# Value matmuls ahead of the output product's piece in steps 10 and 11

## The chip, the cores and the metric

The kernel runs on one core of one Trainium2 chip. The metric is the device time of one execution, in microseconds (us); lower is better. All matmuls take bf16 operands and accumulate in fp32 in PSUM; inputs and output are fp32.

## The reference

Two stages follow each other. The first is an attention between a sequence `x` (8 batches, 8 heads, 512 tokens, 64 wide) and 32 state vectors of each batch and head, in both directions. The second is a gated feed-forward layer on the 4352 rows that come out (8 batches of 512 + 32 rows, 512 wide, hidden width 1536):

```
scores  = x @ state^T / 8            a  = softmax over the 32 states
xread   = a @ state                  (512 rows a batch)
scores2 = state @ x^T / 8            a2 = softmax over the 512 tokens
sread   = a2 @ x                     (32 rows a batch)
rows    = concat(xread, sread) with the heads side by side: 4352 x 512
out     = (sigmoid(rows @ w_gate) * (rows @ w_val)) @ w_out
```

## The kernel before

The program order of each engine is written out by hand. Work is done batch by batch; `step(b, f)` is one of twelve steps of batch `b`, for `b` = 3 to 8, where `b` = 8 stands for the 256 state rows of all batches. Step `f` makes columns `128 f` to `128 f + 127` of the hidden layer:

- Gate and value matmuls (`gv_half`, L360; L363 in batch 8). `xread` is never formed. The product of the states with both weights, `SW`, is made for each batch ahead of time (`sw_six`: state matmuls, L290 and L297; copied out by `sw_cp`, L334), and a step multiplies it by the transposed attention weights `aT`: two matmuls of 512 columns for the gate half (here called G), two for the value half (V).
- `gv_th` (ScalarE, L369) takes the tanh of half the gate; `gv_glu` (VectorE, L374) makes (tanh + 1) times the value half, the glu product; the factor one half is applied at the output.
- The output product of the batch before, `o = b - 1`, is done with Winograd's form of Strassen's method: seven products of blocks instead of eight, each in two pieces a and b of six matmuls of 256 columns (`w_mm`, L437). The sums of glu blocks that it needs are made by `s_sum` (L419), on GpSimd, and one in halves on VectorE at steps 0 and 6. `w_keep` (ScalarE, L442) and `w_add` (VectorE, L445) combine the results, and `w_store` sends them out on SP's queue.
- In steps 0 and 6 TensorE also does the state matmuls for the next batch `nb`, if there is one; the attention of the next batch (`S_mm`, L152, its exponential, sums, transposes) is spread over the other steps.

The pieces that fall into each step are these, "3b4a" being piece 3b and then piece 4a:

```
order = {0: "1a", 1: "1b", 2: "2a", 3: "2b", 4: "6a", 5: "6b", 6: "5a", 7: "5b", 8: "7a7b", 9: "3a", 10: "3b4a", 11: "4b"}
```

A step's matmuls stand as G, pieces, V. In steps 0 and 6 of a batch with a next one they stand as G, V, pieces (`ahead`).

The PSUM tiles of G and V come from one pool of two buffers (`p_gv`), taken in turn, so that in a run of steps G uses one and V the other. Steps 0 and 6 take one tile of the same pool for a state product too. A gate tile is free when `gv_th` has read it, a value tile when `gv_glu` has, a state product when `sw_cp` has. The `tanh` tiles have three buffers, the glu products of a batch two.

What follows the matmuls in steps 10 and 11: `gv_glu`, then one `w_add` on VectorE and one `w_store`. In step 9 `gv_glu` is followed by a `sw_cp` on VectorE. In step 0 VectorE does `s_sum(o, 3, 0)` after `gv_glu`, and GpSimd two `s_sum` that read the glu products of the last six steps of the batch before, the eleventh among them.

Of the kernel before, what the change touches and what calls it, by code (L numbers as in the profile page):

```python
# [16 lines left out]
def kernel(  # L17
# [239 lines left out]
    def rd_mm(b, place):  # L257

        ps = place[0].tile((128, 512), FP, name="rdp", tag=place[1])
        rd = held["rd", b] = ps[:, :2 * D + 2].rearrange("p (e d) -> p e d", e=2)  # L260
        for e in range(2):
            for c in range(4):
                for j in range(4):
                    h, o, Eb = 2 * j + e, rd[j * Ns:(j + 1) * Ns, e], Ebs[b][:, c, e, j * Ns:(j + 1) * Ns]
                    if b > 2:
                        nc.tensor.matmul(o, Eb, xs[:, c, h, :D + 1], start=(c == 0), stop=(c == 3))  # L266
                    else:
                        xh = xhs[b][:, h, c] if b in xhs else xbs[b][:, c, h]
                        nc.tensor.matmul(o[:, :D], Eb, xh, start=(c == 0), stop=(c == 3))
        for e in range(2 if b < 3 else 0):  # L270
            for c in range(4):
                nc.tensor.matmul(rd[:, e, D:], Ebs[b][:, c, e], ones, start=(c == 0), stop=(c == 3))
# [60 lines left out]
    def sw_cp(b, lo, w, e, cp):  # L333
        cp(*sw_left.pop((b, lo, w, e)))  # L334
# [20 lines left out]
    def gv_half(b, f, w, place):  # L355
        n, fs = n_of(b), slice(f * 128, (f + 1) * 128)
        ps = place[0].tile((128, 512), FP, name="gvp", tag=place[1])[:, :n]
        if b < B:
            for g in range(2):
                nc.tensor.matmul(ps, SWs[b][:, g, w, fs], aTs[b][:, :, g], start=(g == 0), stop=(g == 1))  # L360
        else:
            for j in range(4):
                nc.tensor.matmul(ps, (wg, wv)[w][:, j, fs], XS[:, :, j], start=(j == 0), stop=(j == 3))  # L363
        held.setdefault(("gv", b, f), []).append(ps)

    def gv_th(b, f):

        th = held["th", b, f] = fp.tile((128, 512), FP, name="th")[:, :n_of(b)]
        nc.scalar.activation(th, held["gv", b, f][0], AF.Tanh, scale=0.5)  # L369

    def gv_glu(b, f):
        if b not in glus:
            glus[b] = fp.tile((128, NF, n_of(b)), BF, name="glu", bufs=2, padded_shape=(128, NF, 512))
        nc.vector.scalar_tensor_tensor(glus[b][:, f], held["th", b, f], 1.0, held["gv", b, f][1], ALU.add, ALU.mult)  # L374
# [53 lines left out]
    def w_mm(b, k, c):  # L428

        lhs, rhs = prod(b, k)  # L430
        key = {1: 1, 6: 1, 2: 2, 5: 5, 3: 5, 7: 7, 4: 7}[k]
        first = k == key
        if first and c == 0:
            place = OU if key in (1, 5) else SWP
            wps[key] = place[0].tile((128, 2, 256), FP, name="outp", tag=place[1])
        for i in range(NF // 2):
            nc.tensor.matmul(wps[key][:, c], lhs[:, i, c * 128:(c + 1) * 128], rhs[:, i],  # L437
                             start=(first and c == 0 and i == 0), stop=(i == NF // 2 - 1), skip_group_check=True)

    def w_keep(name, key):  # L440
        t = held["w", name] = fp.tile((128, 2, 256), FP, name=name, bufs=1)
        nc.scalar.activation(t, wps[key], AF.Copy, scale=0.5)  # L442

    def w_add(key, name, to):
        nc.vector.scalar_tensor_tensor(to, wps[key], 0.5, held["w", name], ALU.mult, ALU.add)  # L445
# [4 lines left out]
    def p_mm(k, part):  # L450
        c, lo, n = parts[part]
        lhs, rhs = prod(B - 1, k)
        if k == 7:
            wps["p", part] = p_sw.tile((128, 512), FP, name="outp", tag="swp")[:, :n]
        for i in range(NF // 2):
            nc.tensor.matmul(wps["p", part], lhs[:, i, c * 128:(c + 1) * 128], rhs[:, i, lo:lo + n],  # L456
                             start=(k == 7 and i == 0), stop=(i == NF // 2 - 1), skip_group_check=True)
# [9 lines left out]
    def w_res(b, h):  # L467
        if (b, h) not in wres:
            wres[b, h] = fp.tile((128, 2, 512), FP, name="res", bufs=3)
        return wres[b, h]  # L470
# [381 lines left out]
    def sw_six(b, v):  # L852

        if b not in SWs:
            SWs[b] = fp.tile((128, 2, 2, dff), BF, name="SW", bufs=2)
        lo = 768 * v
        for k, places in enumerate((((SWP, GV), (SWP, SWP), (OU, SWP)) if v else ((OU, GV), (SWP, AT), (SWP, SWP)))):
            pss = [p[0].tile((128, 512), FP, name="swp", tag=p[1]) for p in places]
            if k < 2:
                sw_mm(pss, b, k, lo, 512, 0)  # L860
            else:
                sw_pair(pss, b, lo + 512, 256)
            for e in range(2):
                if k < 2:
                    sw_left[b, v, k, e] = (SWs[b][:, e, k, lo:lo + 512], pss[e])
                else:
                    sw_left[b, v, k, e] = (SWs[b][:, e, :, lo + 512:lo + 768], pss[e].rearrange("p (w n) -> p w n", w=2))

    def step(b, f):

        nb, o = (b + 1 if b + 1 < B else None), b - 1
        v = f // 6
        if nb and f in (0, 6):
            if v:
                rd_mm(nb, AT)
            sw_six(nb, v)
            sw_cp(nb, v, 0, 1, act)
            sw_cp(nb, v, 2 * v, 0, act)
        ahead = nb is not None and f in (0, 6)
        gv_half(b, f, 0, GV)  # L880
        gv_th(b, f)
        if ahead:
            gv_half(b, f, 1, GV)
        todo = (order if b < B else last_order)[f]
        for k, c in zip(todo[::2], todo[1::2]):
            if b == B and k == "7":
                for part in range(3):
                    if parts[part][0] == "ab".index(c):
                        p_mm(7, part)
            else:  # L890
                w_mm(o, int(k), "ab".index(c))
        if not ahead:
            gv_half(b, f, 1, GV)
        gv_glu(b, f)

        if f == 1:
            w_keep("V1", 1)
        if f == 5:
            w_keep("U2", 1)
        if nb:  # L900
            if f in (1, 2):
                S_mm(nb, f - 1, AT)
                S_exp(nb, f - 1)
            k = {0: (1, 1), 3: (2, 0), 4: (2, 1), 6: (0, 0), 7: (1, 1), 8: (2, 1)}.get(f)
            if k:
                sw_cp(nb, v, *k, act)

        if f == 0:
            s_sum(o, 3, 0, nc.vector)
        if f == 4:  # L910
            w_add(2, "V1", w_res(o, 0)[:, :, lo_])
        if f == 6:
            s_sum(o, 3, 1, nc.vector)
        if f == 7:
            held["w", "U4"] = fp.tile((128, 2, 256), FP, name="U4", bufs=1)
            w_add(5, "U2", held["w", "U4"])
        if f == 8 and b < B:
            w_add(7, "U4", w_res(o, 1)[:, :, hi_])
        if f == 9 and b == B:
            for part in range(3):  # L920
                p_add("U4", part, 1)
        if f == 10 and b < B:
            w_add(5, "U2", w_res(o, 0)[:, :, hi_])
            w_store(o, 0, nc.sync)
        if f == 11 and b < B:
            w_add(7, "U2", w_res(o, 1)[:, :, lo_])
            w_store(o, 1, nc.sync)
        if nb:
            if f in (1, 9):
                sw_cp(nb, v, 1, 0, vec)  # L930
            if f in (2, 3):
                n_sum(nb, f - 2)
            if f == 5:
                n_mul(nb, 0, nc.vector)
                n_mul(nb, 1, nc.vector)
            if f == 6:
                rd_fin(nb)
                aT_dma(nb, 0)
                aT_dma(nb, 1)
                rd_dma(nb)  # L940

        if f == 0:
            s_sum(o, 0, 1, nc.gpsimd)
            s_sum(o, 1, 1, nc.gpsimd)
            if nb:
                cast_xs(nb, 0, 4)
                cast_xs(nb, 4, 4)
                if nb + 2 < B:
                    load_x(nb + 2, nc.sync)
        if f == 3:  # L950
            if nb:
                at_Eb(nb)
            s_sum(o, 2, 1, nc.gpsimd)
        if f == 6 and nb and nb + 1 < B:
            cast_x(nb + 1, pool, 0, 4)
            cast_x(nb + 1, pool, 4, 4)
            at_xT_dma(nb + 1)
        if f == 8 and b < B:
            for t in range(3):
                s_sum(b, t, 0, nc.gpsimd)  # L960
# [49 lines left out]
```

## Time and profile before

| | |
|---|---|
| median of 3 runs | 218.63 us (217.56 to 218.9) |
| profiled execution | 217.36 us |
| its span, first to last instruction | 215.6 us |
| granted TensorE clock | 1.000 |
| busy: TensorE / VectorE / ScalarE / GpSimd | 208.3 / 147.4 / 125.6 / 130.3 us |

The span is that of the instructions alone; the profiled execution's own time has 1.8 us around it. PE is TensorE's matmuls, PEld its weight loads, DVE is VectorE, ACT is ScalarE, POOL is GpSimd, SP the queue that issues most transfers. A row of the timeline gives the start, the duration, the engine, the line of the kernel, the operation, what it writes and reads, and how many instructions are merged into it; in brackets stands the idle time of the engine before it and what ended it. Matmuls are pipelined: a record lasts longer than the distance to the next one, so the time that a group occupies TensorE is read from one start to the next. In time, step 0 of batches 3 to 7 starts at about 77, 99, 121, 144 and 166 us of the span.

### The profile page before, as it was taken

To read this page: it belongs to the slowest core of one execution; us is meant where nothing else is said; L and a number is where in the kernel's file an instruction comes from. 1 tells how busy PE (TensorE), PEld (TensorE's weight loads), DVE (VectorE), ACT (ScalarE), POOL (GpSimd) and SP (SyncE) were. 2 spreads that over 40 slices of the span, in tenths; PEclk is the share of its full clock that TensorE was granted. 3 is DMA by queue.
4 is the path that set the end of the run, shared out by engine and by line. 5 is a ranking of instruction groups with operands and counts; after the bars stand their busy time and mean duration, and the time that the engine had idled before them with its cause. 6 is when DMAs were issued, how large, how long until landed. Compare 5 with 4: busy or idle time off the path is not lost.

```text
span 215.6 us, 5110 instructions
## 1 busy us (share of the span) xinstructions
PE 208.3 (97%) x1998; PEld 124.1 (58%) x2005; DVE 147.4 (68%) x257; ACT 125.6 (58%) x233; POOL 130.3 (60%) x131
## 2 busy tenths in 40 slices
PE   8899999999999999999999999999999999999991
PEld 2555443444454456675656565656566566788851
DVE  4987987386457559876987698778967657635411
ACT  4778876585575677745775577547763443233220
POOL 8989306269949969483959296729462909360002
PEclk9999999999999999999999999999999999999999
DMA  6999999395699253526832450236011400210053
GB/s 194 203 193 200 198 295 192 96 261 106 89 277 283 47 132 108 170 43 99 286 124 43 97 198 3 49 79 222 0 40 24 191 0 5 120 74 3 0 193 102
DMA packets 40504, 27.14 MB, mean 126 GB/s; under 512 B 23744, under 2 KB 37312, under 8 KB 40480
## 3 DMA queue, kind: packets, MB, share of 16 engines
q1 hardware_dynamic: 30080, 18.95, 31.9%
q0 software_dynamic: 10112, 7.67, 21.1%
q8 instruction: 16, 0.26, 0.5%
q10 hardware_dynamic: 288, 0.20, 0.4%
q14 instruction: 8, 0.07, 0.1%
HBM read 18.35 MB, written 8.91 MB: 126 GB/s over the span
## 4 chain that ended last, share of the span: by engine, by line
PE 91%; DVE 2%; ACT 2%; DMA 2%; issue 1%; POOL 0%; POOLq 0%; SPq 0%; DVEq 0%
PE gvp L360 25%; PE outp L437 24%; PE gvp L348 15%; PE outp L390 12%; PE gvp L363 5%; PE swp L290 3%; PE swp L297 2%; DMA xf<-in_x_dram 2%; PE Sp L152 1%; DVE glu L374 1%; PE rdp L266 1%; PE outp L456 1%; PE warm L484 1%; PE aTp L238 1%; ACT SW L334 0%
## 5 line engine op out<-in xcount | busy, mean ns | idle before, releaser
L374 DVE SCALAR_TENSOR_TENSOR glu<-th,gvp 128x512 bf16<-128x512 f32 (+1 forms) x108 | 70.5, 656 | 48.3 <-ACT th L369 18.2
L369 ACT ACTIVATE th<-gvp 128x512 f32<-128x512 f32 (+1 forms) x108 | 62.0, 576 | 57.6 <-PE gvp L360 34.2
L360 PE MATMUL gvp<-aT,SW 128*128 128x512 bf16 x240 | 64.2, 379 | 0.3
L419 POOL TENSOR_TENSOR Sm<-glu 128x768 bf16<-128x768 bf16 x24 | 39.6, 1651 | 40.3 <-DVE glu L374 27.1
L334 ACT CAST SW<-swp 128x512 bf16<-128x512 f32 x70 | 39.3, 589 | 9.2 <-PE swp L290 7.6
L348 PE MATMUL gvp<-aT,SW 128*128 128x512 bf16 x144 | 35.4, 380 | 0.1
L437 PEld LDWEIGHTS <-Sm 128*128 128x128 bf16 x276 | 27.0, 98 | 10.6
L360 PEld LDWEIGHTS <-SW 128*128 128x128 bf16 x240 | 22.5, 98 | 15.9 <-issue 3.7
L390 PE MATMUL outp<-wo,glu 128*128 128x512 bf16 x113 | 28.2, 379 | 0.4
L437 PE MATMUL outp<-tw,Sm 128*128 128x256 bf16 x204 | 27.0, 273 | 0.0
L437 PEld LDWEIGHTS <-glu 128*128 128x128 bf16 x204 | 20.0, 98 | 7.7
L348 PEld LDWEIGHTS <-SW 128*128 128x128 bf16 x144 | 13.1, 98 | 16.6 <-issue 2.1
L419 POOL TENSOR_TENSOR Sm<-Sm,glu 128x768 bf16<-128x768 bf16 x12 | 20.1, 1671 | 0.9
L437 PE MATMUL outp<-wo,glu 128*128 128x256 bf16 x144 | 19.6, 273 | 0.0
L390 PEld LDWEIGHTS <-glu 128*128 128x128 bf16 x120 | 11.4, 98 | 13.6 <-issue 0.8
L334 DVE CAST SW<-swp 128x512 bf16<-128x512 f32 x26 | 17.5, 682 | 1.7 <-PE swp L297 1.7
L121 POOL CAST xb<-xf 128x1024 bf16<-128x1024 f32 x10 | 10.6, 1088 | 10.8 <-DMA xf<-in_x_dram 9.2
L204 POOL CAST Eb<-E 128x256 bf16<-128x256 f32 x32 | 11.9, 412 | 1.9 <-ACT E L172 1.9
L363 PE MATMUL gvp<-XS,wgv 128*128 128x256 bf16 x96 | 12.6, 273 | 0.0
L419 DVE TENSOR_TENSOR Sm<-glu,Sm 128x768 bf16<-128x768 bf16 x12 | 12.4, 1032 | 0.0
L403 POOL DMA_DIRECT2D out_dram<-res x2 | 1.1, 546 | 18.4 <-ACT res L394 18.4
L255 POOL CAST xs<-xf 128x1024 bf16<-128x1024 f32 x10 | 11.4, 1170 | 0.0
(94 smaller groups left out, 219.7 us busy)
## 6 DMA issues: line engine op xcount, KB each, us to landing
out_dram<-res SPq DMA_DIRECT2D x11, 512.0 KB, 2.9
xf<-in_x_dram SPq DMA_DIRECT2D x4, 1024.0 KB, 7.3
out_dram<-res SPq DMA_DIRECT2D x9, 256.0 KB, 3.4
xf<-in_x_dram POOLq DMA_DIRECT2D x2, 1024.0 KB, 10.0
wo<-in_moe_w_out_dram POOLq DMA_DIRECT2D x3, 512.0 KB, 13.1
xf<-in_x_dram SPq DMA_DIRECT2D x4, 256.0 KB, 3.9
wgv<-in_moe_w_val_dram POOLq DMA_DIRECT2D x4, 256.0 KB, 7.2
wgv<-in_moe_w_gate_dram POOLq DMA_DIRECT2D x4, 256.0 KB, 8.3
```

Of the source, the lines that this page charges most:

```text
L121: cp(xbs[b].rearrange("p c h d -> p h c d")[:, lo:lo + n], (xhs if b in xhs else xfs)[b][:, lo:lo + n])
L204: nc.gpsimd.tensor_copy(Ebs[b][:, c], E1s[b][:, c])
L255: pool(xs.rearrange("p c h d -> p h c d")[:, lo:lo + n, :, :D], xfs[b][:, lo:lo + n])
L334: cp(*sw_left.pop((b, lo, w, e)))
L348: nc.tensor.matmul(ps, SWs[b][:, g, w, fs], aTs[b][:, :, g], start=(g == 0), stop=(g == 1))
L360: nc.tensor.matmul(ps, SWs[b][:, g, w, fs], aTs[b][:, :, g], start=(g == 0), stop=(g == 1))
L363: nc.tensor.matmul(ps, (wg, wv)[w][:, j, fs], XS[:, :, j], start=(j == 0), stop=(j == 3))
L369: nc.scalar.activation(th, held["gv", b, f][0], AF.Tanh, scale=0.5)
L374: nc.vector.scalar_tensor_tensor(glus[b][:, f], held["th", b, f], 1.0, held["gv", b, f][1], ALU.add, ALU.mult)
L390: nc.tensor.matmul(ops[b, c], glus[b][:, f, c * 128:(c + 1) * 128], wo[:, f], start=(f == 0), stop=(f == NF - 1))
L419: eng.tensor_tensor(Sm[:, t, i], a, c, op)
L437: nc.tensor.matmul(wps[key][:, c], lhs[:, i, c * 128:(c + 1) * 128], rhs[:, i], start=(first and c == 0 and i == 0), stop=(i == NF // 2 - ...
```

## The change

One line of `step` is changed:

```diff
         if nb and f in (0, 6):
             if v:
                 rd_mm(nb, AT)
             sw_six(nb, v)
             sw_cp(nb, v, 0, 1, act)
             sw_cp(nb, v, 2 * v, 0, act)
-        ahead = nb is not None and f in (0, 6)
+        ahead = nb is not None and f in (0, 6, 10, 11)
         gv_half(b, f, 0, GV)
         gv_th(b, f)
         if ahead:
             gv_half(b, f, 1, GV)
         todo = (order if b < B else last_order)[f]
         ...
         if not ahead:
             gv_half(b, f, 1, GV)
         gv_glu(b, f)
```

In steps 10 and 11 of a batch that has a next one the value matmuls stand ahead of the pieces: G10, V10, 3b, 4a, then G11, V11, 4b. `nb` is the next batch below 8, so these are batches 3 to 6; batch 7 has `nb = None` and keeps its order, though the change is described as one of batches 3 to 7. The built programs have the same instructions on every engine; on TensorE 80 rows of 4012 stand in another place, in four batches, and the orders of the other engines and queues are the same.

## The prediction

> **What bounds the kernel now.** I read the page first (busy time by engine, granted clock), then the chain of waits, then the timeline around the changed steps in batches 4 and 6.
>
> ```profile
> span 215.6 us, 5110 instructions
> PE 208.3 (97%) x1998; PEld 124.1 (58%) x2005; DVE 147.4 (68%) x257; ACT 125.6 (58%) x233; POOL 130.3 (60%) x131
> PEclk9999999999999999999999999999999999999999
> PE 91%; DVE 2%; ACT 2%; DMA 2%; issue 1%; POOL 0%; POOLq 0%; SPq 0%; DVEq 0%
> ```
>
> TensorE is busy 97% of the span at full clock, and 91% of the chain that ended last is TensorE. The matmuls stay the same, so the change can only add or remove time in which TensorE stands still. The timeline of batch 4, from step 9's value matmuls to the next batch's step 0 (start, duration, engine):
>
> ```profile
> 117.35 1.03 PE L360 MATMUL gvp<-aT,SW 128*128 128x512 bf16 x4
> 118.05 0.69 DVE L374 SCALAR_TENSOR_TENSOR glu<-th,gvp 128x512 bf16<-128x512 f32 x1 [0.23 <-PE gvp L360]
> 118.22 0.82 PE L437 MATMUL outp<-wo,Sm 128*128 128x256 bf16 x6
> 118.42 0.60 ACT L369 ACTIVATE th<-gvp 128x512 f32<-128x512 f32 x1 [0.92 <-PE gvp L360]
> 118.87 0.82 PE L437 MATMUL outp<-tw,glu 128*128 128x256 bf16 x6
> 119.53 1.03 PE L360 MATMUL gvp<-aT,SW 128*128 128x512 bf16 x4
> 120.23 0.69 DVE L374 SCALAR_TENSOR_TENSOR glu<-th,gvp 128x512 bf16<-128x512 f32 x1 [0.88 <-PE gvp L360]
> 120.39 0.82 PE L437 MATMUL outp<-tw,glu 128*128 128x256 bf16 x6
> 120.83 0.68 DVE L445 SCALAR_TENSOR_TENSOR res<-outp,U 128x512 f32<-128x512 f32 x1
> 121.04 0.59 PE L360 MATMUL gvp<-aT,SW 128*128 128x512 bf16 x2
> 121.57 0.62 PE L290 MATMUL swp<-wgv,sTc 64*32 64x512 bf16 x16
> 121.75 0.69 DVE L374 SCALAR_TENSOR_TENSOR glu<-th,gvp 128x512 bf16<-128x512 f32 x1 [0.23 <-PE gvp L360]
> 122.01 0.40 PE L297 MATMUL swp<-wgv,sTc 64*32 64x512 bf16 x8
> 122.05 1.07 ACT L334 CAST SW<-swp 128x512 bf16<-128x512 f32 x2 [0.87 <-PE swp L290]
> 122.49 1.02 PE L360 MATMUL gvp<-aT,SW 128*128 128x512 bf16 x4
> 123.12 0.60 ACT L369 ACTIVATE th<-gvp 128x512 f32<-128x512 f32 x1
> ```
>
> I write G and V for a step's pair of gate and value matmuls. The row of four at 117.35 is V9 and G10, that at 119.53 is V10 and G11, the two at 121.04 are V11. A pair occupies TensorE for 0.43 us (117.35 to 118.22 holds two), a piece of six for 0.65 (118.22 to 118.87). TensorE runs here without a pause, since between one V and the next stand a piece and a G. Each glu product starts 0.70 after its V starts (117.35 to 118.05, 119.53 to 120.23) and takes 0.69; TensorE starts on what it frees 0.05 later (121.75 + 0.69 = 122.44, then G0 at 122.49).
>
> Three places where TensorE stands still today bear on the change. At step 0, G0 comes 0.48 after the last eight state matmuls begin, while at step 6, with nothing to wait for, it is 0.34, so 0.14 is waiting for glu 11. Later in step 2, V2 should follow its piece after 0.65 and comes 0.10 late, because glu 1 is late behind a VectorE sum that took 1.88:
>
> ```profile
> 110.27 0.62 PE L290 MATMUL swp<-wgv,sTc 64*32 64x512 bf16 x16
> 110.71 0.40 PE L297 MATMUL swp<-wgv,sTc 64*32 64x512 bf16 x8
> 111.05 1.04 PE L360 MATMUL gvp<-aT,SW 128*128 128x512 bf16 x4
> 124.23 1.64 POOL L419 TENSOR_TENSOR Sm<-Sm,glu 128x768 bf16<-128x768 bf16 x1
> 124.40 1.88 DVE L419 TENSOR_TENSOR Sm<-glu,Sm 128x768 bf16<-128x768 bf16 x1
> 126.19 0.82 PE L437 MATMUL outp<-wo,glu 128*128 128x256 bf16 x6
> 126.21 0.68 DVE L374 SCALAR_TENSOR_TENSOR glu<-th,gvp 128x512 bf16<-128x512 f32 x1
> 126.94 0.59 PE L360 MATMUL gvp<-aT,SW 128*128 128x512 bf16 x2
> ```
>
> The third is in batch 7 and is shown below.
>
> **The change part by part.** The condition asks for a next batch, so it reaches batches 3 to 6 and not 7: four batches, eight steps. Only TensorE's order changes; the instructions of VectorE, ScalarE, GpSimd and the DMA queue keep theirs, so no transfer passes another.
>
> *Step 10, the new wait.* The order becomes G10, V10, 3b, 4a. The gate and value tiles alternate between two buffers, so V10 writes the one that V9 filled and glu 9 must have read. Before, 12 matmuls (1.31) stood between G10 and V10 and hid that; now G10 alone stands there. V10 is due at 117.35 + 0.87 = 118.22. Glu 9 ends at 118.05 + 0.69 = 118.74, so V10 starts at 118.79: **0.57 us of new waiting**. Behind V10 in TensorE's order are the twelve ready matmuls of 3b and 4a, which could have run. Both sides of this cost: glu 9 cannot start sooner than the 0.70 that every row shows, and VectorE had been idle 0.23 before it, so nothing lengthens it either; I keep 0.57 to 0.60.
>
> *Step 11, no wait.* 3b and 4a now run 119.22 to 120.53, G11 follows, V11 is due at 120.96. It needs glu 10, which runs 0.70 after V10, 119.49 to 120.18; free. G11 needs tanh 10, done at 119.02. The second res addition, on VectorE behind glu 10, moves from 120.83 to about 120.10. 4b runs 121.40 to 122.05.
>
> *What comes back at step 0.* The state matmuls start at 122.15 instead of 121.57 (I keep the 0.10 that separates them from V11 now, 121.04 + 0.43 = 121.47), 0.58 later. Glu 11 now runs 121.66 to 122.35, before G0, due 0.78 after the state matmuls as at step 6, 122.93. So G0's wait of 0.14 goes and G0 is 0.44 later. ScalarE's two copies and tanh 0 move by 0.58: tanh 0 ends at 124.30, and G1, which needs it, is due at 123.99 + 0.44 = 124.43. That is 0.08 of cover; if it is gone, each of three batches loses about 0.1 more.
>
> *What comes back at step 2.* GpSimd's two sums start after glu 11, at nearly today's times. VectorE's sum still ends 0.41 after the second GpSimd sum (124.23 + 1.64 = 125.87; 124.40 + 1.88 = 126.28), so glu 1 is set by V1, and V2, due 0.44 later, finds it done. The 0.10 goes. **Batches 3, 4 and 5: 0.57 - 0.14 - 0.10 = 0.33 each, 0.99 in all.** The bounds: 0.33 if both waits go, 0.57 if neither.
>
> *Batch 6 into batch 7.* There is no next batch's state work in batch 7, so nothing stands between 4b and G0:
>
> ```profile
> 162.02 1.03 PE L360 MATMUL gvp<-aT,SW 128*128 128x512 bf16 x4
> 162.72 0.69 DVE L374 SCALAR_TENSOR_TENSOR glu<-th,gvp 128x512 bf16<-128x512 f32 x1 [0.23 <-PE gvp L360]
> 166.41 0.69 DVE L374 SCALAR_TENSOR_TENSOR glu<-th,gvp 128x512 bf16<-128x512 f32 x1 [0.23 <-PE gvp L360]
> 167.18 1.65 POOL L419 TENSOR_TENSOR Sm<-glu 128x768 bf16<-128x768 bf16 x1 [3.97 <-DVE glu L374]
> 167.23 1.03 PE L360 MATMUL gvp<-aT,SW 128*128 128x512 bf16 x4
> 167.96 0.69 DVE L374 SCALAR_TENSOR_TENSOR glu<-th,gvp 128x512 bf16<-128x512 f32 x1 [0.26 <-PE gvp L360]
> 168.56 0.68 DVE L419 TENSOR_TENSOR Sm<-glu,Sm 128x768 bf16<-128x768 bf16 x1
> 168.91 1.84 POOL L419 TENSOR_TENSOR Sm<-Sm,glu 128x768 bf16<-128x768 bf16 x1
> 170.26 1.03 PE L360 MATMUL gvp<-aT,SW 128*128 128x512 bf16 x4
> 171.13 0.82 PE L437 MATMUL outp<-wo,glu 128*128 128x256 bf16 x6
> 171.32 0.69 DVE L374 SCALAR_TENSOR_TENSOR glu<-th,gvp 128x512 bf16<-128x512 f32 x1 [1.19 <-PE gvp L360]
> 172.06 1.02 PE L360 MATMUL gvp<-aT,SW 128*128 128x512 bf16 x4
> ```
>
> V10 moves to 163.46, V11 to 165.63, V0 of batch 7 (now 167.23) to 167.81: the whole 0.57 to 0.58 arrives. But glu 11 does not move (166.33 instead of 166.41), so GpSimd's sums run 167.10 to 168.75 and 168.83 to 170.47. VectorE's sum comes after glu 0: 167.81 + 0.73 = 168.54, and 0.60 later, 169.14. Today it comes at 168.56, ahead of the second GpSimd sum, and costs 0.68; now it comes 0.31 behind its start, as in batch 5's row of 1.88. It then ends at 170.47 + 0.41 = 170.88, glu 1 runs 170.81 to 171.49, and V2, due at 170.26 + 0.58 = 170.84, starts at 171.54: **0.70 more**. Its bounds are 0 (row 168.56) and 0.70 (row 124.40); I take 0.70, since GpSimd is 0.31 ahead.
>
> The Trainium skill (SBUF — State Buffer, Who interferes with whom) says a VectorE instruction with two SBUF inputs and a GpSimd one that reads SBUF exclude each other, and that issue order decides who blocks. The trace agrees in both orders: 1.88 behind GpSimd, 0.68 ahead of its second sum. By that rule the term would be the 0.70; against it, were the engines to share, nothing.
>
> Today V3 waits 0.28 (171.13 + 0.65 = 171.78, but 172.06), since glu 2 started 171.32 instead of 170.96; no released wait explains that. After the change V3 is due at 173.06 and a glu 2 on time frees it at 172.98: I count the 0.28 as returned; the bounds are 0 and 0.28.
>
> **Sum:** 0.99 + 0.57 + 0.70 - 0.28 = **1.98 us more**. On the profiled execution, 217.36 with a span of 215.6, that gives 219.3; the median of the runs shown, 218.63, lies 1.27 above it, and I predict that median: 218.63 + 1.98 = **220.6**.
>
> **The rivals.**
>
> *The late glu 2 stays.* The same sum without the 0.28: 2.26, 220.9. For it: VectorE's order is unchanged. Against it: it occurs once in five batches.
>
> *No collision in batch 7.* If VectorE's sum slips in ahead, 1.28, or 1.56 with a late glu 2: 219.9 to 220.2. Against it: the 0.31.
>
> *The waits do not come back.* If ScalarE's copies, tanh 0 or glu 1 slide along with the state matmuls, the 0.42 and 0.30 of steps 0 and 2 are replaced by waits of like size: 2.70, and 2.98 with a late glu 2, 221.3 to 221.6. For it: the cover of 0.08 at G1.
>
> *Faster.* The mechanism is glu 11 ahead of G0: steps 0 and 2 return 0.72, V3 0.28, together 1.00. It decides only if V10 waits less than 0.25 a time (1.00 / 4), so glu 9 would have to start 0.38 after V9, where the rows say 0.70. Free of any wait it gives 218.63 - 1.00 = 217.6, half a percent faster.
>
> *The change does nothing.* If V10 found a third buffer, only the order would differ, 218.6. The value tile's pool has two.
>
> **How the numbers follow.** A measurement here can tell about 1%, 2.19 us, from no change. Chances: the sum of 1.98 0.38, with the late glu 2 0.22, waits not returned 0.22, no collision 0.11, faster 0.04, nothing 0.03. The first lies 0.2 below the bound, while the runs shown differ by 1.3; I give 0.17 of its 0.38 to slower, of the second 0.15, of the third all: slower 0.54, and 0.04 to faster, which leaves 0.42 within 1%. Range: from the lowest run shown plus the smallest of the likely sums, 217.56 + 1.28 = 218.8, to the largest, 2.98, on the highest, 218.9 + 2.98 = 221.9. All in it but the last two rivals are slower than before.
>
> **What would show it.** Right: in batches 3 to 6 a pause of 0.57 before V10, with glu 9 on the chain; G0 0.34 after the last state matmuls; V2 on time in batches 4 to 6; in batch 7 a VectorE sum near 1.7 and V2 late. Wrong: V10 without a pause, or 3b running during it; G0 still at 0.48; a sum of 0.68 in batch 7. A total below 218.8 would mean that V10's buffer is free sooner than I read.

## The result and the profile after

| | before | after |
|---|---|---|
| median | 218.31 us (4 runs, 217.56 to 218.9) | 220.84 us (4 runs, 220.56 to 224.26) |
| ratio after to before | | 1.011, 95% interval 1.0072 to 1.0149 |

The forecast was 220.6 us. A second series of the same two kernels gave 1.0057 (1.001 to 1.0103). The ratios leave out runs over 1.5% above the fastest of their kernel. The totals of both kernels spread by several microseconds, mostly because of a pause in the work before batch 3, which the change does not touch and to which the last experiments come; the first profile of the changed kernel had that pause (222.5 us of span). So the rows below are from the second profile (span 218.1), and I measure in every profile a stretch free of the pause, from the start of G0 of batch 3 to the start of the last matmul. It takes 132.87 us before (from 77.88 to 210.75 us of the span) and 135.31 after (77.88 to 213.19), 2.44 more; in the first profile after it is 135.30. The last matmul starts 4.8 and 4.9 us before the end of the span.

The first row is the group of the gate and value matmuls on the page of the second profile. The last column is the idle time of TensorE before them; before the change it was 0.3:

```profile
L360 PE MATMUL gvp<-aT,SW 128*128 128x512 bf16 x240 | 64.4, 379 | 2.4 <-DVE glu L374 2.3
```

Among the waits it stands with the number of times and the longest:

```profile
PE gvp L360 <- DVE glu L374: 2.3, 5, 0.6
```

These are five waits: four of V10 and one of V2 in batch 7. The timeline of batch 4, from V9 to the next batch's G0, is this:

```profile
117.71 1.03 PE L360 MATMUL gvp<-aT,SW 128*128 128x512 bf16 x4
118.41 0.69 DVE L374 SCALAR_TENSOR_TENSOR glu<-th,gvp 128x512 bf16<-128x512 f32 x1 [0.23 <-PE gvp L360]
119.15 0.59 PE L360 MATMUL gvp<-aT,SW 128*128 128x512 bf16 x2 [0.42 <-DVE glu L374]
119.58 0.82 PE L437 MATMUL outp<-wo,Sm 128*128 128x256 bf16 x6
120.89 1.03 PE L360 MATMUL gvp<-aT,SW 128*128 128x512 bf16 x4
121.52 0.60 ACT L369 ACTIVATE th<-gvp 128x512 f32<-128x512 f32 x1 [2.15 <-PE gvp L360]
121.75 0.82 PE L437 MATMUL outp<-tw,glu 128*128 128x256 bf16 x6
122.15 0.69 DVE L374 SCALAR_TENSOR_TENSOR glu<-th,gvp 128x512 bf16<-128x512 f32 x1 [1.01 <-ACT th L369]
122.94 0.40 PE L297 MATMUL swp<-wgv,sTc 64*32 64x512 bf16 x8
123.27 0.60 PE L360 MATMUL gvp<-aT,SW 128*128 128x512 bf16 x2
```

V9 and G10 start at 117.71 and take 0.86; V10 is due at 118.57 and starts at 119.15, 0.05 after glu 9 ends (118.41 + 0.69 = 119.10): a pause of 0.58. The row prints 0.42, since it counts from the end of the record before, not from its start. Nothing waits at G11 and V11, and G0 follows the last state matmuls after 0.33 instead of 0.48. One row differs from the forecast, glu 11 at 122.15: what ended the idle time before it is no longer a value matmul but tanh 11. V11 starts at 120.89 + 0.43 = 121.32, so glu 11 comes 0.83 after it, not 0.70.

Batch 7, from V11 of batch 6 on:

```profile
167.52 0.69 DVE L374 SCALAR_TENSOR_TENSOR glu<-th,gvp 128x512 bf16<-128x512 f32 x1 [1.01 <-ACT th L369]
168.28 1.64 POOL L419 TENSOR_TENSOR Sm<-glu 128x768 bf16<-128x768 bf16 x1 [4.03 <-DVE glu L374]
170.00 1.64 POOL L419 TENSOR_TENSOR Sm<-Sm,glu 128x768 bf16<-128x768 bf16 x1
170.20 1.86 DVE L419 TENSOR_TENSOR Sm<-glu,Sm 128x768 bf16<-128x768 bf16 x1
170.38 1.03 PE L360 MATMUL gvp<-aT,SW 128*128 128x512 bf16 x4
171.24 0.82 PE L437 MATMUL outp<-wo,glu 128*128 128x256 bf16 x6
171.98 0.67 DVE L374 SCALAR_TENSOR_TENSOR glu<-th,gvp 128x512 bf16<-128x512 f32 x1
172.70 1.02 PE L360 MATMUL gvp<-aT,SW 128*128 128x512 bf16 x4 [0.65 <-DVE glu L374]
173.56 0.82 PE L437 MATMUL outp<-wo,glu 128*128 128x256 bf16 x6
173.75 0.69 DVE L374 SCALAR_TENSOR_TENSOR glu<-th,gvp 128x512 bf16<-128x512 f32 x1 [1.10 <-PE gvp L360]
174.50 0.81 PE L360 MATMUL gvp<-aT,SW 128*128 128x512 bf16 x3
```

VectorE's sum comes 0.20 after the start of GpSimd's second one and takes 1.86 instead of 0.68. V2 is due at 171.24 + 0.65 = 171.89 and starts at 172.70, 0.81 late. Glu 2 starts 1.05 after V2 once more, and V3 is late by 0.28 (0.29 from these rounded rows) as before.

### The profile page after: what moved, and what is told of

Read it like the earlier page. It is cut to its first block, busy times and chain, and to the rows that moved or that the text cites. A ratio compares the mean times of both kernels' runs of the same rounds, so it can differ in the third digit from the quotient of the medians.

```text
span 222.5 us, 5110 instructions
## 1 busy us (share of the span) xinstructions
PE 210.2 (94%) x1998; PEld 124.3 (56%) x2005; DVE 149.7 (67%) x257; ACT 125.5 (56%) x233; POOL 130.1 (58%) x131
## 4 chain that ended last, share of the span: by engine, by line
PE 86%; DVE 6%; ACT 2%; DMA 2%; issue 2%; POOL 0%; POOLq 0%; SPq 0%; DVEq 0%
PE gvp L360 23%; PE outp L437 23%; PE gvp L348 14%; PE outp L390 11%; PE gvp L363 5%; PE swp L290 3%; DVE glu L374 3%; DVE ab L231 2%; PE swp L297 2%; DMA xf<-in_x_dram 2%; PE Sp L152 1%; PE warm L484 1%; PE rdp L266 1%; PE outp L456 1%; PE xTp L137 1%
## 5 line engine op out<-in xcount | busy, mean ns | idle before, releaser
L419 POOL TENSOR_TENSOR Sm<-glu 128x768 bf16<-128x768 bf16 x24 | 40.4, 1682 | 47.3 <-DVE glu L374 33.2
L360 PE MATMUL gvp<-aT,SW 128*128 128x512 bf16 x240 | 64.4, 379 | 2.4 <-DVE glu L374 2.3
L348 PE MATMUL gvp<-aT,SW 128*128 128x512 bf16 x144 | 36.5, 387 | 2.8 <-DVE glu L374 2.7
L390 PE MATMUL outp<-wo,glu 128*128 128x512 bf16 x113 | 29.1, 388 | 0.4
L121 POOL CAST xb<-xf 128x1024 bf16<-128x1024 f32 x10 | 10.1, 1039 | 10.9 <-DMA xf<-in_x_dram 9.4
L394 ACT ACTIVATE res<-outp 128x512 f32<-128x512 f32 x10 | 6.0, 597 | 12.1 <-PE outp L390 12.1
```

The costliest lines, as they stand in the source:

```text
L121: cp(xbs[b].rearrange("p c h d -> p h c d")[:, lo:lo + n], (xhs if b in xhs else xfs)[b][:, lo:lo + n])
L390: nc.tensor.matmul(ops[b, c], glus[b][:, f, c * 128:(c + 1) * 128], wo[:, f], start=(f == 0), stop=(f == NF - 1))
L419: eng.tensor_tensor(Sm[:, t, i], a, c, op)
```

## The experiments

For each I give the stretch from G0 of batch 3 to the last matmul, which was 132.87 us before the change and which a profile resolves to some hundredths, and the ratio of the totals to those of the kernel before where it was measured. Edits are cut from the code and shown against the changed kernel where nothing else is said.

**The changed kernel again.** 

> The changed kernel once more, for a second profile and a tighter ratio. Theory (four waits of V10 on glu 9 of 0.58, the waits of 0.14 at G0 and 0.10 at V2 gone in three batches, and V2 of batch 7 0.81 late behind the VectorE sum): 2.31 - 0.43 - 0.29 + 0.81 = 2.4 us over before, ratio 1.011. Rival (part of the 2.5 us measured first comes from the start of the kernel, where the first profile of after stood still for 2.8 us at 69 us): 1.5 to 2, and that pause would be seen again.

The stretch took 135.31, 2.44 more than before, against 2.40 expected. The ratio was 1.0057 (1.001 to 1.0103), not 1.011. The pause at 69 us was absent from this profile, and the stretch was the same with it (135.30) and without it, so the cost is not from there.

**Step 10 alone.**

```diff
-        ahead = nb is not None and f in (0, 6, 10, 11)
+        ahead = nb is not None and f in (0, 6, 10)
```

> V ahead in step 10 alone; step 11 as before. Theory (each change from V behind the pieces to V ahead of them costs one wait for the glu product before, 0.58): V10 waits 0.58 four times, G0 and V2 keep their small waits, and since glu 11 moves with TensorE the GpSimd sums do too, so no collision in batch 7: 2.3 us over before. Rival (the two steps share the cost): about 1.2. Rival (most of the cost is the collision): 1.5 or less.

The stretch took 135.15, 2.28 more than before; the ratio was 1.0124 (1.0051 to 1.0196). V10 pauses 0.58 in all four batches, G0 keeps its 0.48, V2 of batches 4 to 6 its 0.09, and there is no collision in batch 7.

**Step 11 alone.**

```diff
-        ahead = nb is not None and f in (0, 6, 10, 11)
+        ahead = nb is not None and f in (0, 6, 11)
```

> V ahead in step 11 alone; step 10 as before. Theory: the same wait, now V11 on glu 10, 0.58 four times; glu 11 is early against G0, so the waits of 0.14 and 0.10 go and the collision in batch 7 comes (0.70): 2.31 - 0.43 - 0.29 + 0.70 = 2.3 us over before, as much as both steps together. Rival (the steps add up): about 1.2, or about 0 if step 10 alone bears the cost.

The stretch took 135.17, 2.30 more than before; the ratio was 1.0146 (1.0082 to 1.021). The timeline of batch 4 with step 11 alone:

```profile
123.61 1.03 PE L360 MATMUL gvp<-aT,SW 128*128 128x512 bf16 x4
124.31 0.69 DVE L374 SCALAR_TENSOR_TENSOR glu<-th,gvp 128x512 bf16<-128x512 f32 x1 [0.89 <-PE gvp L360]
125.05 0.59 PE L360 MATMUL gvp<-aT,SW 128*128 128x512 bf16 x2 [0.42 <-DVE glu L374]
125.48 0.82 PE L437 MATMUL outp<-tw,glu 128*128 128x256 bf16 x6
```

The same pause of 0.58 now stands before V11 (due 123.61 + 0.86 = 124.47, starts 125.05). Either step costs as much as both: the price is paid once, where V moves from behind the pieces to ahead of them, because there alone two V's stand closer than glu needs: 0.86 us, where 0.70 to its start, 0.69 for it and 0.05 to the next matmul make 1.44.

**Another buffer for V10.** The step's value tile goes to the attention tiles' PSUM buffer.

```diff
         if ahead:
-            gv_half(b, f, 1, GV)
+            gv_half(b, f, 1, AT if f == 10 else GV)
```

> As the change, but the value tile of step 10 lies in the PSUM buffer of the attention tiles, which is idle in steps 7 to 11. Theory (V10 waits for nothing but its buffer): no pause at V10, and G11 and V11 find theirs free; G0 and V2 waits gone, glu 11 earlier against TensorE, so the collision in batch 7 stays at 0.81: -0.43 - 0.29 + 0.81 = 0.1 us, no difference from before. Rival (V10 is late for another reason, such as the tanh or TensorE's own order): 2.4 us over before.

The stretch took 133.02, 0.15 more than before; the ratio was 0.9957 (0.991 to 1.0004). The timeline of batch 4:

```profile
121.67 1.46 PE L360 MATMUL gvp<-aT,SW 128*128 128x512 bf16 x6
122.37 0.69 DVE L374 SCALAR_TENSOR_TENSOR glu<-th,gvp 128x512 bf16<-128x512 f32 x1 [0.23 <-PE gvp L360]
122.96 0.82 PE L437 MATMUL outp<-wo,Sm 128*128 128x256 bf16 x6
```

V9, G10 and V10 are one row of six; 3b starts 1.29 later, three pairs without a pause, while glu 9 still runs. So V10 waited for its buffer and for nothing else. The collision in batch 7 remained.

**VectorE's sum later in batch 7.**

```diff
-        if f == 0:
+        if f == (0 if b < B - 1 or b == B else 3):
             s_sum(o, 3, 0, nc.vector)
```

> As the change, but in batch 7 VectorE's sum of glu blocks is issued after glu 3 instead of after glu 0, where GpSimd's three sums are nearly done. Theory (the sum is held behind a GpSimd sum and makes glu 1 and V2 late): V2 of batch 7 on time, 2.40 - 0.81 = 1.6 us over before. Rival (V2 of batch 7 is late for another reason): 2.4.

The stretch took 134.22, 1.35 more than before; the ratio was 1.0055 (1.0004 to 1.0106). Glu 1, glu 2 and the GpSimd sums of batch 7:

```profile
173.19 1.64 POOL L419 TENSOR_TENSOR Sm<-Sm,glu 128x768 bf16<-128x768 bf16 x1
174.27 0.69 DVE L374 SCALAR_TENSOR_TENSOR glu<-th,gvp 128x512 bf16<-128x512 f32 x1 [0.80 <-PE gvp L360]
174.79 1.64 POOL L419 TENSOR_TENSOR Sm<-glu 128x768 bf16<-128x768 bf16 x1
175.09 1.03 PE L360 MATMUL gvp<-aT,SW 128*128 128x512 bf16 x4
175.79 0.69 DVE L374 SCALAR_TENSOR_TENSOR glu<-th,gvp 128x512 bf16<-128x512 f32 x1 [0.83 <-PE gvp L360]
```

Glu products run beside GpSimd's sums at their usual 0.69, V2 (175.09) is on time: 0.81 is back. Beyond what was expected, the 0.28 of the late glu 2 is gone as well (175.09 + 0.70 = 175.79): 2.44 - 0.81 - 0.28 = 1.35.

**Without batch 6.**

```diff
-        ahead = nb is not None and f in (0, 6, 10, 11)
+        ahead = nb is not None and f in ((0, 6, 10, 11) if nb < B - 1 else (0, 6))
```

> The change in batches 3 to 5 only; batch 6 as before. Theory: three times 0.58 - 0.14 - 0.10, and nothing in batch 7: 1.0 us over before. Rival (all four batches cost alike): 1.8.

The stretch took 133.95, 1.08 more than before; the ratio was 1.0044 (0.9987 to 1.01). Batch 6 bears 2.44 - 1.08 = 1.36, the others 0.36 each.

**V10 between the two pieces.** V10 behind 3b and ahead of 4a, step 11 as in the change.

```diff
-        ahead = nb is not None and f in (0, 6, 10, 11)
+        ahead = nb is not None and f in (0, 6, 11)
+        mid = nb is not None and f == 10
         ...
                 w_mm(o, int(k), "ab".index(c))
+            if mid and k == "3":
+                gv_half(b, f, 1, GV)
-        if not ahead:
+        if not ahead and not mid:
```

> V10 between 3b and 4a, V11 ahead of 4b. Theory: a piece and a gate pair (1.09 us with V's own 0.43 making 1.52) stand between V9 and V10 and again between V10 and V11, more than the 1.44 that the glu product needs, so no pause; the small waits at G0 and V2 go, the collision in batch 7 stays: 0.1 us over before. Rival (moving V ahead costs in itself): 1.2 to 2.4.

The stretch took 133.00, 0.13 more than before; the ratio was 1.005 (1.0006 to 1.0094). The stretch is as expected. The ratio of the totals is higher, and this run's profile shows time outside the stretch: it has the pause before batch 3, and 5.9 us instead of 4.8 from its last matmul to the end. The timeline of batch 4, with V9 and G10 in the first row and V10 in the fourth:

```profile
121.75 1.03 PE L360 MATMUL gvp<-aT,SW 128*128 128x512 bf16 x4
122.45 0.69 DVE L374 SCALAR_TENSOR_TENSOR glu<-th,gvp 128x512 bf16<-128x512 f32 x1 [0.23 <-PE gvp L360]
122.61 0.82 PE L437 MATMUL outp<-wo,Sm 128*128 128x256 bf16 x6
123.27 0.59 PE L360 MATMUL gvp<-aT,SW 128*128 128x512 bf16 x2
123.70 0.82 PE L437 MATMUL outp<-tw,glu 128*128 128x256 bf16 x6
```

V10 follows 3b without a pause, 0.13 after glu 9 ends (122.45 + 0.69 = 123.14), and V11 does not wait either. So it was the distance between two V's and not their being ahead of pieces.

**Buffer and sum together.** This run has the edits of the fourth and the fifth run.

> The value tile of step 10 in the attention tiles' buffer, and batch 7's VectorE sum after glu 3. Theory: no pause at V10, none at G0 or V2, no collision: 0.43 + 0.29 = 0.7 us under before, ratio 0.997. Rival (something fixed takes up what is gained): no difference.

The stretch took 131.92, 0.95 less than before, against 0.7 expected. The totals do not tell it from no change: the ratio was 0.9972 (0.9928 to 1.0017), the lowest total 216.2 us against 217.54, and the median of all runs 219.74 against 219.35. The page has no idle time before the gate and value matmuls any more:

```profile
L360 PE MATMUL gvp<-aT,SW 128*128 128x512 bf16 x240 | 63.8, 379 | 0.0
```

The gain of 0.95 is 0.43 of G0, 0.29 of V2 and 0.28 of the late glu 2, within 0.05; the last of these was not expected.

**Why glu 2 is late.** One more memset in the start.

```diff
     nc.vector.memset(ones, 1.0)
+    nc.vector.memset(ones, 1.0)
```

> The change with one more tiny VectorE instruction (a second memset of the ones column, 128x1) in the start of the kernel. It asks only why glu 2 of batch 7 starts 1.05 us after V2 instead of 0.70. Theory (the 0.35 belongs to a place in VectorE's list of instructions): with the list one longer, glu 2 is on time and another instruction may be late. Rival (it belongs to what glu 2 does beside the GpSimd sums): glu 2 at 1.05 as in every profile in which VectorE's sum stands two places ahead of it.

V2 and glu 2 of batch 7:

```profile
182.49 1.02 PE L360 MATMUL gvp<-aT,SW 128*128 128x512 bf16 x4 [0.64 <-DVE glu L374]
183.19 0.69 DVE L374 SCALAR_TENSOR_TENSOR glu<-th,gvp 128x512 bf16<-128x512 f32 x1 [0.75 <-PE gvp L360]
```

Glu 2 started 0.70 after V2 and V3 was on time; the stretch was 135.03, 0.28 less than with the change. So the 0.35 belongs to a place in VectorE's list of instructions and not to glu 2 or to GpSimd beside it. This one execution took 229.42 us in all, for G0 of batch 3 came at 87.67 instead of 77.88; whether the memset has to do with that was not tested.

The traces show a little more of that place. VectorE's list also has entries that only wait for other engines. Counted with these, the late start lies between the 319th and the 320th entry in every profile that has it, where the 320th is glu 2. In the run with one more memset, and wherever VectorE's sum was moved, the 320th entry is itself a wait for a value matmul, which would hide 0.35. One transfer of 8192 bytes on the queue that the page calls instruction moves along with the list: it starts at 171.99 before the change, 0.67 after the late glu 2, and at 181.92 in the run with one more memset, ahead of glu 2. That suggests that the list is loaded in blocks and that the late start lies at the edge of one; no run tests it, and what happens there stays open.

**The sum later, without the change.** This is the edit of the fifth run in the kernel before.

> The kernel before, with batch 7's VectorE sum after glu 3 instead of after glu 0. Theory (in the kernel before the sum comes in ahead of the second GpSimd sum and holds nobody up): V2 as before, and only the late glu 2 may go: from G0 of batch 3 to the end 137.4 to 137.7 us against 137.7. Rival (the move itself is worth the 0.9 us that it brings to the changed kernel): 136.8.

The stretch took 132.59, 0.28 less than before: the late glu 2 alone. The move is worth the other 0.81 only where the change has brought the collision about.

**What spreads the totals.** Two profiles of the changed kernel differ before batch 3. VectorE's two normalising products and GpSimd's instructions, first in the profile without the pause:

```profile
65.12 2.54 POOL L121 CAST xb<-xf 128x1024 bf16<-128x1024 f32 x2 [1.59 <-PE gvp L348]
66.08 2.12 DVE L231 TENSOR_TENSOR ab<-E,ri 128x512 bf16<-128x512 f32 x2
67.62 3.54 POOL L412 TENSOR_TENSOR tw<-wo,tw 128x1536 bf16<-128x1536 bf16 x1
```

and then in the one with it:

```profile
64.92 2.03 POOL L121 CAST xb<-xf 128x1024 bf16<-128x1024 f32 x2 [1.47 <-PE gvp L348]
66.00 4.98 DVE L231 TENSOR_TENSOR ab<-E,ri 128x512 bf16<-128x512 f32 x2
66.91 3.54 POOL L412 TENSOR_TENSOR tw<-wo,tw 128x1536 bf16<-128x1536 bf16 x1
72.04 0.91 PE L348 MATMUL gvp<-aT,SW 128*128 128x512 bf16 x2 [2.66 <-DVE glu L374]
```

The row of casts in each holds two. Without the pause VectorE comes at 66.08, while GpSimd's first cast still runs (until 66.16), gets in ahead of the second, and its other product ahead of GpSimd's long sum. With the pause it comes at 66.00, after the first cast's end (65.97), waits for the second cast, and its other product for the long sum; the glu product behind it and a value matmul wait 2.7 us. All 14 profiles fit this: in the eight in which the first product starts before the end of the first cast, the other takes 0.90 to 1.52 us; in five it starts 0.04 to 0.19 after that end, and the other takes 3.57 or 3.58; in the run with one more memset it starts 1.57 after, and the two take 5.1.

The pause alone does not make the whole spread. In the profile with it the granted clock was 0.57 from 72 to 76 us of the span, right behind the pause, and 1.00 from 60 to 72 and from 76 to 90, and G0 of batch 3 came 4.43 later than in the profile without the pause (82.31 against 77.88). By an estimate, 4 us at 0.57 lose 1.7 (4 x 0.43), which with the 2.8 of the products accounts for the 4.43. In the profile of step 11 alone the pause was there and the clock stayed at 1.00.

Issuing the first product one step earlier takes the race away; the edit is against the kernel before:

```diff
+        if f == 4:
+            n_mul(nb, 0, nc.vector)
         if f in (3, 4):
             n_sum(nb, f - 3)
-        elif f == 5:
-            n_mul(nb, 0, nc.vector)
```

> The kernel before, with VectorE's first normalising product for batch 3 (n_mul, in step 2 of the loop before batch 3) issued one step earlier, while GpSimd is idle. It asks why runs of one kernel spread by 4 us: in profiles that start batch 3 at 78 us the two products take 2.1 us, in those that start it at 81 to 84 us 5.0, the second behind a GpSimd sum of 3.5. Theory (which engine is first at 66.0 us is a matter of less than 0.1 us and decides 2.8 us): the slow group of runs goes, the lowest time stays near 217.5 and the median falls to within 1 us of it. Rival (the spread has another source, such as the start or the transfers): the spread stays.

The first product now starts while GpSimd is idle, and the other ahead of the second cast:

```profile
64.52 0.69 DVE L231 TENSOR_TENSOR ab<-E,ri 128x512 bf16<-128x512 f32 x1
66.62 0.90 DVE L231 TENSOR_TENSOR ab<-E,ri 128x512 bf16<-128x512 f32 x1
```

The twelve runs lay between 217.39 and 218.77 with a median of 217.9; the kernel before, on the same chip, gave 23 between 217.32 and 223.08 with a median of 220.58. The spread goes as expected; the ratio, 0.9977 (0.9944 to 1.001), hardly moves, for the reason given with the result.

**All three edits.**

> Value tile of step 10 in the attention tiles' buffer, batch 7's VectorE sum after glu 3, and the normalising product one step earlier. Theory: 0.95 less from G0 of batch 3 to the last matmul as in the run without the last edit, and no 2.8 us pause before batch 3: lowest near 216.2, median below 217.5, ratio 0.99 or less. Rival (the spread stays): median near 219.5.

The stretch took 131.92 again; the median was 217.1 (12 runs, 216.79 to 219.88) and the ratio 0.9949 (0.9907 to 0.9992). The stretch and the median are as expected; the lowest total is 0.6 above the 216.2 and the ratio above the 0.99 that were expected. This is the fastest version by its median: 3.5 us below the kernel before (217.1 against 220.58), most of it the pause, and 0.8 below the kernel before with the last edit alone (217.9), near the 0.95 of the stretch.

## Why the prediction was right or wrong

*The new wait: right.* It was predicted as 0.57 and measured as 0.58 in each of the four batches, released 0.05 after glu 9. The run with another buffer shows that the buffer makes it, and the run with V10 between the pieces shows that a distance of 1.52 between two V's suffices.

*No wait in step 11: right.* But glu 11 was wrong by 0.13. The forecast took 0.70 after V for its start, read from steps in which the tanh had long been done. With V11 right behind G11 the tanh is the later of the two, and glu 11 starts 0.83 after V11.

*What comes back at steps 0 and 2: right.* G0's 0.14 and V2's 0.10 are gone in three batches, and ScalarE's 0.08 of cover at G1 held. Batches 3 to 5 cost 0.33 by the sum; the run without batch 6 gives 0.36.

*The collision in batch 7: the mechanism right, the term mis-sized.* 0.70 was predicted, 0.81 measured. With glu 11 late by 0.13, GpSimd's sums are late too, and so is all that VectorE's sum and glu 1 wait for. In the run with step 11 alone V11 waits, tanh 11 is done in time, glu 11 comes at 0.70, and V2 is 0.68 late, close to the prediction. The fifth run shows that the sum does it. The Trainium skill (SBUF — State Buffer, Who interferes with whom) lets whichever of the two starts first keep the other out; both the batch 7 rows and the pair of profiles before batch 3 agree, with 1.86 against 0.68 and 4.98 against 2.12 us.

*The late glu 2: wrong.* I counted its 0.28 as returned: no wait explained why glu 2 was late, so I let it start on time after the change. It came again in full, 1.05 after V2; the run with one more memset shows that the late start goes with a place in VectorE's list, which the change leaves as it was. The rival with the late glu 2, at 2.26, was the right one, and its reason, that VectorE's order is unchanged, as well. With the terms as measured it is 4 x 0.58 - 3 x 0.14 - 3 x 0.10 + 0.81 = 2.41; the stretch gave 2.44, the medians 2.53.

*The total: nearer than the terms, by luck.* The forecast was 220.6 and the median 220.84. The two errors have one sign, so the sum of 1.98 was 0.46 below the stretch's 2.44. I added it to a median before of 218.63, and the one beside the result is 218.31, so a start 0.32 too high made up for most of what the sum lacked. The second series, at 1.0057, shows how far totals of this kernel can mislead: a pause of 2.8 us, decided by about 0.1 us, lies in both kernels.

## What to carry to other kernels

In a ring of two buffers count the distance from one writer to the next, not the order within a step: moving a write forward shortens that distance once, where the order changes, and costs nothing where it stays even or long enough: 0.86 us cost 0.58 here, 1.52 nothing. Where two engines share something that one holds for a whole instruction, ask who now comes first after every shift of a few tenths: VectorE's sum came 0.35 ahead of GpSimd's before and 0.20 behind it after, which was worth 0.8 us, and about 0.1 us was worth 2.8 before batch 3. Measure an effect of one percent over a stretch of the trace that leaves such races out.

## What was not expected of the hardware

One VectorE instruction, glu 2 of batch 7, started 0.35 us later after its matmul than the other glu products (1.05 instead of 0.70), in every profile in which it had the same place in VectorE's list, and on time in all where the list was one longer or the sum before it had been moved. VectorE's arrival 0.08 us before the end of a GpSimd cast in one profile and 0.04 after it in another made the difference between 2.12 and 4.98 us for the same two products. And in the changed kernel's profile with the pause the granted clock was 0.57 for the 4 us behind it, in another run's with the same pause 1.00.
